# Convolution, MLP and GELU on one core: the 512-token blocks moved from two 64x128 TensorE tiles to four 64x64 tiles, with W_out stationary and the result transposed by VectorE

## The chip, the cores and the metric

One core of a Trainium2 chip. The metric is the device time of one execution in microseconds (us). All runs were correct, unless it is said otherwise, and of the fast state but for one each in the medians of e1 and e2. A ratio is the mean time of one kernel's fast runs over the mean of the other's from the same rounds, so it isn't quite the ratio of the medians quoted beside it.

## The reference

```python
# x: (8, 4096, 192), weight: (8 heads, 7 taps); softmax over the taps
w = softmax(weight, axis=-1)
out = einsum('hk,bskhg->bshg', w, causal_windows(x, 7))   # 24 channels per head
t = out.reshape(32768, 192)
h = t @ w_in                                              # 192 -> 2048
g = 0.5 * h * (1 + erf(h / sqrt(2)))
return g @ w_out                                          # 2048 -> 192, float32
```

## The kernel before

The tokens run in two halves of 16,384: half 0 lives on partitions 0 to 63, half 1 on 64 to 127, and the two row tiles of TensorE (64 rows each) work side by side. A block is 256 (six small ones at the start) or 512 tokens (29 blocks) of *each* half. VectorE transposes the input and does the seven taps for all blocks but two, two blocks ahead of their use. TensorE runs the first product of block n interleaved with the second product of block n-1; ScalarE does the Gelu.

```python
WS = [256] * 6 + [512] * ((HALF - 1536) // 512)     # block sizes
hp = [pst("hp%d" % i, [128, 2 * TB]) for i in range(2)]   # first product, 2 x 2 PSUM banks
ob = [pst("ob%d" % i, [128, 1024]) for i in range(2)]     # second product, 2 x 2 PSUM banks

def mm1(n, i):              # 128 of the 2048 hidden channels: 3 passes over 64 input channels
    ...
    for p in range(NP):
        for hf in range(2):                          # the two row tiles
            r = slice(64 * hf, 64 * hf + 64)
            ins = t.matmul(hp[u % 2][:, hf * TB + cc * w : ...],       # out: 128 x 512
                           win[r, p * F + wcols(hf, f0) : ... + 128],  # stationary 64 x 128
                           xc[n % 2][r, p * TB : p * TB + w],          # streamed 64 x 512
                           start=(p == 0), stop=(p == NP - 1), tile_position=(64 * hf, 0))

def mm2(m, g, ph, i):       # 4 groups of 2 x 128 tokens, 2 phases, 16 hidden chunks
    ...
    for hf in range(2):
        sub = ph ^ hf                                # row tiles swap banks between phases
        ins = t.matmul(ob[gg % 2][:, 512 * sub : 512 * sub + C],
                       gT[m % 2][r, c0 : c0 + 128],                    # stationary: tokens
                       wout[r, CH[i] * C : (CH[i] + 1) * C],           # streamed: 192 columns
                       start=..., stop=..., tile_position=(64 * hf, 0))

for i in range(NSL[n]):     # a slot: one piece of mm1(n), then its share of mm2(n - 1)
    mm1(n, i)
    for un in todo[a0:a1]: mm2(n - 1, *un)

def evac(e, m, g):          # VectorE: tensor_copy of 128 x (2 x 192) from ob to osb
def store(e, m):            # 4 DMAs per block, pieces of 3072 bytes
```

## Time and profile before

| | before |
|---|---|
| device time, median of 3 | 691.83 us (691.72 to 692.56) |
| span of the profiled run | 690.5 us |
| share busy: TensorE, VectorE, ScalarE | 99%, 80%, 77% |
| TensorE instructions (weight loads + matmuls) | 2 x 11,652 |
| steady 512-block, start to start | 20.92 us |

A group line of the profile gives the source line, the engine, the operation, output <- inputs, the shapes, how often; then total busy time and the mean of one in ns; then idle time before it and what ended it. A timeline line is start, length, engine, line, what, how many merged. Durations of matmuls overlap: what a matmul costs TensorE is the distance to the next start.

### The profile page before, as it was taken

Reading aid. Unit: us, or ns where it says so; the run is one execution under the profiler, and the core shown is the slowest. Engines: PE = TensorE matmul, PEld = TensorE weight load, DVE = VectorE, ACT = ScalarE, POOL = GpSimd, SP = SyncE. Lnnn points to the kernel's source line nnn. Section 1 sums busy time; section 2 is a strip of 40 time slices with the busy share of each in tenths; the row PEclk is TensorE's granted clock in tenths of the full one; section 3 lists DMA queues with packets and bytes.
Section 4 is the critical chain, followed back from the end, with each engine's and each line's share of the span. In section 5 each row is a group of like instructions: output and inputs, shape, how many; then the busy total and the mean of one; then the engine's idle time right before and its main releaser. Section 6 shows DMA issues by size and latency. Waiting matters only on the chain.

```text
span 690.5 us, 25644 instructions
## 1 busy us (share of the span) xinstructions
PE 682.3 (99%) x11652; PEld 506.3 (73%) x11652; DVE 555.7 (80%) x942; ACT 532.0 (77%) x536; POOL 45.1 (7%) x97
## 2 busy tenths in 40 slices
PE   8999999999999999999999999999999999999997
PEld 4899667777777777777777777777777777777777
DVE  6999977788977779878789777789877798777701
ACT  6788987777777777777777777777777777777771
POOL 7110000000000000000000000000000000000000
PEclk9999999999999999999999999999999999999999
DMA  9667844335554345653345553355544356521023
GB/s 198 134 149 165 205 111 109 88 88 132 138 137 100 74 106 138 139 135 88 82 112 138 138 122 87 84 124 138 138 101 93 86 136 139 135 50 40 11 48 93
DMA packets 24236, 78.15 MB, mean 113 GB/s; under 512 B 7232, under 2 KB 12480, under 8 KB 20416
## 3 DMA queue, kind: packets, MB, share of 16 engines
q1 hardware_dynamic: 19600, 72.24, 44.9%
q0 software_dynamic: 3792, 3.50, 2.9%
q8 instruction: 91, 1.49, 1.0%
q10 hardware_dynamic: 736, 0.78, 0.4%
q14 instruction: 17, 0.14, 0.1%
HBM read 52.90 MB, written 25.17 MB: 113 GB/s over the span
## 4 chain that ended last, share of the span: by engine, by line
PE 95%; DMA 2%; ACT 1%; POOL 1%; issue 0%; DVE 0%
PE ob L647 48%; PE hp L615 46%; DMA wout<-in_moe_w_out_dram 1%; ACT gT L547 1%; DMA xin<-in_x_dram 1%; POOL xin L204 0%; POOL xTb L302 0%; ACT osb L194 0%; ACT L496 0%; DVE osb L196 0%; DVE xT L413 0%
## 5 line engine op out<-in xcount | busy, mean ns | idle before, releaser
L547 ACT ACTIVATE gT<-hp 128x1024 bf16<-128x1024 f32 x512 | 522.8, 1023 | 139.7 <-PE hp L615 139.7
L647 PEld LDWEIGHTS ob<-wout,gT 64*128 64x128 bf16 x8192 | 352.7, 94 | 112.8 <-DMA wout<-in_moe_w_out_dram 1.3
L647 PE MATMUL ob<-wout,gT 64*128 64x192 bf16 x8192 | 420.7, 243 | 1.2 <-DMA wout<-in_moe_w_out_dram 1.1
L615 PE MATMUL hp<-xc,win 64*128 64x512 bf16 (+1 forms) x3360 | 415.5, 358 | 1.0 <-ACT gT L547 0.7
L443 DVE SCALAR_TENSOR_TENSOR acc<-xT,wcol,acc 128x512 f32<-128x512 f32 (+1 forms) x495 | 318.7, 710 | 0.0
L615 PEld LDWEIGHTS hp<-xc,win 64*128 64x128 bf16 x3360 | 154.6, 94 | 61.0 <-ACT gT L547 1.9
L196 DVE COPY osb<-ob 128x384 f32<-128x384 f32 x116 | 63.9, 551 | 124.2 <-PE ob L647 124.2
L443 DVE SCALAR_TENSOR_TENSOR xc<-xT,wcol,acc 128x512 bf16<-128x512 f32 (+1 forms) x99 | 65.1, 713 | 0.0
L413 DVE STREAM_TRANSPOSE xT<-xin 128x512 f32<-128x512 f32 (+1 forms) x105 | 61.3, 635 | 2.9 <-issue 2.1
L308 POOL COPY xT<-xT 128x558 f32<-128x558 f32 x33 | 21.5, 652 | 587.5 <-DVE xT L413 587.5
L436 DVE TENSOR_SCALAR acc<-xT,wcol 128x512 f32<-128x512 f32 (+1 forms) x99 | 56.2, 619 | 1.1
L291 POOL COPY xT<-xT 128x18 f32<-128x18 f32 x30 | 11.5, 384 | 1.1 <-DVE xc L396 1.1
L560 PE MATMUL hp<-warm 128*128 128x512 bf16 x16 | 5.4, 516 | 1.3 <-DVE warm L328 1.3
L576 PE MATMUL ob<-xTb,dg 64*64 64x256 bf16 x84 | 5.3, 271 | 1.1 <-ACT xTb L510 1.0
L576 PEld LDWEIGHTS ob<-xTb,dg 64*64 64x64 bf16 x84 | 4.3, 106 | 2.3 <-ACT xTb L510 1.5
L194 ACT ACTIVATE osb<-ob 128x384 f32<-128x384 f32 x12 | 5.8, 486 | 0.0
L560 PEld LDWEIGHTS hp<-warm 128*128 128x128 bf16 x16 | 1.9, 126 | 4.3 <-issue 2.4
L204 POOL DMA_DIRECT2D xin<-in_x_dram x10 | 5.0, 513 | 0.0
L258 POOL DMA_DIRECT2D win<-in_moe_w_in_dram x6 | 3.9, 655 | 0.0
L373 DVE COPY win<-win 64x768 bf16<-64x768 bf16 (+1 forms) x6 | 3.2, 532 | 0.2
L510 ACT ACTIVATE xTb<-xT 128x256 bf16<-128x256 f32 x3 | 1.1, 417 | 2.9 <-DVE xT L413 2.9
L302 POOL CAST xTb<-xT 128x186 bf16<-128x186 f32 x6 | 2.4, 402 | 2.7 <-DVE xT L413 2.7
(29 smaller groups left out, 14.1 us busy)
## 6 DMA issues: line engine op xcount, KB each, us to landing
xin<-in_x_dram SPq DMA_DIRECT2D x116, 380.0 KB, 6.8
out_dram<-osb SPq DMA_DIRECT2D x112, 192.0 KB, 3.0
out_dram<-osb SPq DMA_DIRECT2D x56, 48.0 KB, 2.2
xin<-in_x_dram SPq DMA_DIRECT2D x12, 188.0 KB, 3.9
xin<-in_x_dram POOLq DMA_DIRECT2D x10, 188.0 KB, 5.8
wout<-in_moe_w_out_dram POOLq DMA_DIRECT2D x1, 768.0 KB, 10.3
win<-in_moe_w_in_dram POOLq DMA_DIRECT2D x4, 96.0 KB, 4.4
win<-in_moe_w_in_dram POOLq DMA_DIRECT2D x2, 192.0 KB, 4.8
```

Of the source, the lines that this page charges most:

```text
L194: e.activation(out=dst, in_=src, func=AF.Copy).then_inc(S_EVA)
L196: e.tensor_copy(dst, src).then_inc(S_EV)
L291: g.tensor_copy(dst, ap(xT[(n - 1) % 2], WS[n - 1] + 31, [[NP * XW, 128], [XW, NP], [32, HB]],),).then_inc(S_HALO)
L308: g.tensor_copy(ap(t, 1, [[NP * tw, 128], [tw, NP], [32, HB], [1, 31]]), ap(t, WS[n], [[NP * tw, 128], [tw, NP], [32, HB], [1, 31]]),).the ...
L413: v.transpose(ap(xT[n % 2], p * XW + HL, [[NP * XW, 128], [1, w]]), ap(xin[n % NX], 64 * p, [[TB // 32 * D, 128], [D, w // 32], [1, 32]],) ...
L436: ins = v.tensor_scalar(a, src, wk, None, ALU.mult)
L443: ins = v.scalar_tensor_tensor(dst, src, wk, a, op0=ALU.mult, op1=ALU.add)
L547: a.activation(out=ap(gT[n % 2], i * c * 2 * w, dst), in_=ap(hp[u % 2], 0, src), func=AF.Gelu,).then_inc(S_GELU)
L560: t.matmul(hp[1][:, 0:512], warm[:, 0:128], warm[:, :])
L576: ins = t.matmul(b[r, o : o + w], dg[r, d0 : d0 + 64], xTb[PC[n]][r, x0 : x0 + w], start=(k == KS - 1), stop=(k == 0), tile_position=(64 * ...
L615: ins = t.matmul(hp[u % 2][:, hf * TB + cc * w : hf * TB + cc * w + w], win[r, p * F + wcols(hf, f0) : p * F + wcols(hf, f0) + 128], xc[n ...
L647: ins = t.matmul(ob[gg % 2][:, 512 * sub : 512 * sub + C], gT[m % 2][r, c0 : c0 + 128], wout[r, CH[i] * C : (CH[i] + 1) * C], start=(ph == ...
```

## The change

In the second product the roles swap for blocks 6 to 33: W_out becomes stationary (64 hidden x 64 output channels, every third channel), and 512 tokens are streamed through it. Four 64x64 tiles run at once: two row tiles (hf) by two column tiles (h, the token half). The result has channels on partitions, so VectorE evacuates it with a 32x32-block transpose into the row layout. The first product of blocks 7 to 34 is cut into 64-column tiles as well, so that the mode of the array stays the same. Four PSUM banks become a ring. The intent is to stream 512 columns instead of 192 per weight load. Below, a pair is the two matmuls that start together on two tiles, a quad the four on four tiles.

```diff
+            fw = 64 if M0 < n <= M1 else 128
+            for fo in range(0, 128, fw):
+                ins = t.matmul(
+                    hp[u % 2][fo : fo + fw, o : o + w],
+                    win[r, f1 : f1 + fw], ...
+                    tile_position=(64 * hf, fo),
 ...
+        UPLO = [(1, 0), (0, 2), (2, 1)]           # pass -> output third of each row tile
+            def mm2_t(m, ps, i):                  # 3 passes x 16 hidden chunks
+                if i == 0: ...                    # a bank of the ring must be free
+                for hf in range(2):
+                    j = UPLO[ps][hf]
+                    for h in range(2):
+                        ins = t.matmul(
+                            bank(ring(m, j), slice(64 * h, 64 * h + 64), w),
+                            ap(wout, 64 * hf * NF * C + CH[i] * C + j,
+                               [[NF * C, 64], [NP, 64]]),          # every third channel
+                            gT[m % 2][r, c0 : c0 + w],             # 512 tokens
+                            ..., tile_position=(64 * hf, 64 * h),
+            SHARE = [3, 3, 3, 3, 4, 3, 3, 3, 3, 4, 3, 3, 3, 3, 2, 2]
 ...
+        def evac_t(v, m, j):
+            v.transpose(
+                ap(osb[m % 2], j, [[8 * C, 128], [C // 2, TB // 32], [NP, 32]]),
+                bank(ring(m, j)),
+            ).then_inc(S_EV)
+        # places in VectorE's program: (n + 2, 18), (n + 3, 6), (n + 3, 9)
 ...                                               # store: pieces of 3072 -> 384 bytes
+                        [[mb * C, 32], [C, mb], [1, C // 2]],
 ...                                               # Gelu reads and writes in plain order
```

## The prediction

> **What bounds the kernel now.** I read the page first (busy shares, slices, chain of waits, groups), then the timeline of one steady block on PE and on VectorE.
>
> ```profile
> PE 682.3 (99%) x11652; PEld 506.3 (73%) x11652; DVE 555.7 (80%) x942; ACT 532.0 (77%) x536; POOL 45.1 (7%) x97
> ...
> PEclk9999999999999999999999999999999999999999
> ...
> PE 95%; DMA 2%; ACT 1%; POOL 1%; issue 0%; DVE 0%
> PE ob L647 48%; PE hp L615 46%; DMA wout<-in_moe_w_out_dram 1%; ACT gT L547 1%; DMA xin<-in_x_dram 1%; POOL xin L204 0%; POOL xTb L302 0%; ACT osb L194 0%; ACT L496 0%; DVE osb L196 0%; DVE xT L413 0%
> ```
>
> TensorE is the bound from end to end: 95% of the chain, halved between the first product (hp, L615) and the second (ob, L647), at a granted clock of 9 tenths or more in every slice. A busy PE is not a PE at its peak, so the question is whether there is waste between its starts. The groups give the shapes, the timeline the rhythm:
>
> ```profile
> L647 PE MATMUL ob<-wout,gT 64*128 64x192 bf16 x8192 | 420.7, 243 | 1.2 <-DMA wout<-in_moe_w_out_dram 1.1
> L615 PE MATMUL hp<-xc,win 64*128 64x512 bf16 x2784 | 376.3, 376 | 0.1
> ```
>
> ```profile
> 406.13 0.82 PE L647 MATMUL ob<-wout,gT 64*128 64x192 bf16 x16
> 406.79 0.81 PE L615 MATMUL hp<-xc,win 64*128 64x512 bf16 x6
> 407.44 0.82 PE L647 MATMUL ob<-wout,gT 64*128 64x192 bf16 x16
> 408.10 0.81 PE L615 MATMUL hp<-xc,win 64*128 64x512 bf16 x6
> ```
>
> Here the starts matter, not the durations (matmuls overlap). 16 second-product matmuls occupy 0.66 us: they run as pairs on the two row tiles, so 8 pairs at 82.5 ns. Six first-product matmuls occupy 0.65 us: 3 pairs, and the trace's single starts stand 216 ns apart. These two shapes separate rate and overhead: 320 more columns take 133.5 ns more, 0.417 ns a column (2.4 columns per ns), and what is left is 82.5 - 192 x 0.417 = 2.5 ns per pair. So TensorE already streams one column per cycle without holes; its only waste is 2.5 ns per pair: 3% of the second product, 1.2% of the first. A steady 512-block is 16 slots of 0.648 + 0.660, 20.93 us; block starts in the trace are 20.92 us apart, 27 times running.
>
> ```profile
> 405.03 1.02 ACT L547 ACTIVATE gT<-hp 128x1024 bf16<-128x1024 f32 x1 [0.28 <-PE hp L615]
> 406.34 1.02 ACT L547 ACTIVATE gT<-hp 128x1024 bf16<-128x1024 f32 x1 [0.28 <-PE hp L615]
> ```
>
> ```profile
> 416.00 3.39 DVE L443 SCALAR_TENSOR_TENSOR acc<-xT,wcol,acc 128x512 f32<-128x512 f32 x5
> 419.31 2.07 DVE L443 SCALAR_TENSOR_TENSOR xc<-xT,wcol,acc 128x512 bf16<-128x512 f32 x3
> 421.30 0.55 DVE L196 COPY osb<-ob 128x384 f32<-128x384 f32 x1
> 425.30 0.56 DVE L196 COPY osb<-ob 128x384 f32<-128x384 f32 x1 [3.45 <-PE ob L647]
> ```
>
> ScalarE waits 0.28 us for PE before each Gelu. VectorE has the convolution for the next block done at 421.4 and then waits 3.45 us for PE's last group: about 3.7 us of slack per block. Neither sets the pace.
>
> **What the Trainium skill says.** "TensorE: Matmul & The Clock Gate", section "Wait — 56ns, not 53.3ns?", gives N/2.4 + about 2.5 ns per warm matmul; the trace agrees (216 and 82.5 ns), and shows that two tiles side by side pay it once per pair. "TensorEngine Tiling (Array Packing)", sections "Tiling Modes" and "Gotcha 2", lists 64x64 as four independent tiles, says that a change of mode drains the engine, and that column tiling excludes Fast Weight Load. The trace before has 64x64 only in the opening convolution, two tiles of four: 107 ns a weight load against 94 at 64x128. When weights of one tile were loaded twice after a pause, the second load began about 28 ns after the first at 64x64, 15 ns at 64x128; I take these as the real occupancy of the load. The first page also says (Part 3, "The mechanism") that a load overlaps a running matmul only in another row group. The trace disagrees: in the second product each load starts 2 ns after the same row tile's matmul and the next still starts at 82.5 ns. "DMA: Bandwidth & Descriptors", "Specifications", puts line rate at 512 bytes or more a piece; the new stores are 384.
>
> **The change part by part.** It touches PE blocks 7 to 34, 28 of them.
>
> Second product. Removed per block: 4 groups x 2 phases x 16 chunks = 128 pairs with 192 columns, 128 x 82.5 = 10.56 us. Added: 3 passes x 16 chunks = 48 quads with 512 columns. If four tiles pay 2.5 ns once, 48 x 216 = 10.37 us. The streamed columns are the same (128 x 192 = 48 x 512), so this exchange saves only overhead: 80 x 2.5 = 0.20 us a block.
>
> First product. 48 pairs become 48 quads: 48 x 216 again. Nothing gained; it keeps the mode constant.
>
> Weight loads. A quad needs four of 64 columns in 216 ns; even wholly serial, 4 x 28 = 112 ns (estimate), hidden. Instructions to feed: 8 per 216 ns, 27 ns each, against 4 per 82.5 ns, 21 ns each, which the queue sustains today.
>
> VectorE. Removed: 4 copies x 551 = 2.20 us. Added: 3 transposes out of PSUM. The 512-wide transpose in SBUF took 680; PSUM source and steps of three words on the write side add something, I take 0.75: 2.25 us. Even. What moves is when it waits: the first transpose of a block stands before the last six convolution steps of the next input, and waits for pass 2. By the new shares pass 2 ends with slot 9: 10 x 0.648 + 32 x 0.216 = 13.4 us into the block, so 7.3 us remain. Signal 0.25 + transpose 0.75 + six steps at about 0.68 (3.39/5) = 5.1 us. Slack falls from 3.7 to about 2.2 us, still off the path. A bank is also free in time: pass 2 of the next block needs the second transpose, 6.9 us into that block; VectorE is there after 0.75 + six steps + three transposes and three first taps (3.6) + 0.7, about 9 us after pass 2 ended, 2 us into the block.
>
> ScalarE. Same 1023 ns; it reads plainly now. The tightest slots have two quads of the second product: 0.648 + 0.432 = 1.08 us, still over 1.02, and only twice per block.
>
> Stores. Per block 4 x 64 pieces of 3 KB become 4 x 512 of 384 bytes. The trace's W_out load is 2048 packets of 384 bytes at a median 51 ns: 2048 x 51 / 16 = 6.5 us of each engine per block, replacing 256 x 210 / 16 = 3.4. DMA share goes from about 0.48 to 0.63. Loads have over a block to land.
>
> Ends. One drain at each mode change, below 0.5 us. The last block's second group needs banks that two late transposes must clear: about 1.6 us after the passes end against 1.3 us of other work, some 0.3 us lost.
>
> Sum: 28 x 0.20 = 5.6 us saved, 0.3 to 0.5 given back, 5.2 net: 691.8 - 5.2 = 686.6, 0.75% faster.
>
> **The rivals.** (1) Four tiles don't stream freely: loads in a shared row group hold the neighbour's matmul, or the 2.5 ns is paid per column tile. For: no run here has two column tiles at once, and Fast Weight Load is lost. Against: loads hide in the same row tile at 82.5 ns, a tighter spot. 2.5 ns more per quad x 96 quads x 28 = 6.7 us, which just eats the gain (about 693); one exposed load of 28 ns per quad gives 75 us (about 760). (2) VectorE becomes the bound, if the transpose with steps of three words writes at half rate, 1.2 us each: the deadline becomes 5.6 of 7.3 us, still met, about 687. It takes 2.9 us per transpose to break it; at 3.5 us, TensorE would lose 0.6 us a block, about 17 us. (3) DMA: 160 ns per store packet would be 20 us per block, beyond capacity beside the loads, and the kernel would stretch to some 27 us a block (over 850). Packets of 768 bytes on the same kind of queue took some 47 ns, so I hold this for very unlikely. (4) Slow issue of stores with 512 pieces: SP waits 18 us in most blocks and could absorb several us per store.
>
> **Range and chances.** The gain has a hard ceiling: only overhead can go, so below 685 there is hardly anything, and 2% (678) would need 14 us where all the second product's overhead is 28 x 0.32 = 9 us. The failures are one-sided and mostly large. Predicted 686.6 us, range 685.0 to 696.0; faster by over 2%: 0.02, within 2%: 0.88, slower by over 2%: 0.10.
>
> **What would show it.** Right: block starts 20.72 us apart; 512-column matmuls in fours, quads 216 ns apart; PE idle as small as now; VectorE waiting some 2 us per block, at the transposes; DMA share near 0.6. Wrong: quads over 218 ns apart (rival 1); PE waiting for VectorE at a block's start (rival 2); transposes waiting on stores, or VectorE on loads of x (rival 3).

## The result and the profile after

| | before | after |
|---|---|---|
| device time, median of 4 | 691.78 us | 687.21 us (686.39 to 687.63) |
| ratio | | 0.9932 (0.9914 to 0.9949) |
| span of the profiled run | 690.5 us | 685.8 us |
| steady block, start to start | 20.920 us | 20.720 us |
| TensorE instructions | 2 x 11,652 | 2 x 12,548 |

The change is 0.7% faster, within 2%. The outputs are right. The page of the changed kernel, the lines that answer to those of before (busy shares; chain by line; the groups of both products, of the new weight loads and of the transposing evacuation):

```profile
PE 677.9 (99%) x12548; PEld 409.1 (60%) x12548; DVE 563.0 (82%) x914; ACT 532.0 (78%) x536; POOL 45.3 (7%) x97
...
PE hp L681 47%; PE ob L745 42%; PE ob L712 5%; DMA wout<-in_moe_w_out_dram 2%; ACT gT L610 1%; DMA xin<-in_x_dram 1%; POOL xin L256 0%; POOL xTb L366 0%; ACT osb L225 0%; ACT L556 0%; DVE osb L245 0%; DVE osb L227 0%; DVE xT L476 0%
...
L681 PE MATMUL hp<-xc,win 64*64 64x512 bf16 (+2 forms) x6048 | 418.5, 366 | 1.0 <-ACT gT L610 0.7
L745 PE MATMUL ob<-gT,wout 64*64 64x512 bf16 x5376 | 366.3, 376 | 0.0
...
L745 PEld LDWEIGHTS ob<-gT,wout 64*64 64x64 bf16 x5376 | 172.1, 118 | 123.0
L245 DVE STREAM_TRANSPOSE osb<-ob 128x512 f32<-128x512 f32 x84 | 74.0, 883 | 104.4 <-PE ob L745 104.4
```

TensorE is still the whole chain (47 + 42 + 5%) and still never idle in the steady part. What changed is the rhythm. The timeline of the changed kernel on TensorE:

```profile
405.68 0.82 PE L681 MATMUL hp<-xc,win 64*64 64x512 bf16 x12
406.33 0.82 PE L745 MATMUL ob<-gT,wout 64*64 64x512 bf16 x12
406.98 0.82 PE L681 MATMUL hp<-xc,win 64*64 64x512 bf16 x12
407.62 1.03 PE L745 MATMUL ob<-gT,wout 64*64 64x512 bf16 x16
```

Twelve matmuls, three quads, take 0.65 us from start to start: 216 ns a quad, for both products; the second product's slot was 0.66 us before. In the single starts of the trace every steady block is 20.720 us apart, 26 times in a row, against 20.920: 0.200 us a block.

VectorE in the same stretch of the changed kernel:

```profile
415.40 0.91 DVE L245 STREAM_TRANSPOSE osb<-ob 128x512 f32<-128x512 f32 x1 [3.00 <-PE ob L745]
416.18 2.01 DVE L506 SCALAR_TENSOR_TENSOR acc<-xT,wcol,acc 128x512 f32<-128x512 f32 x3
418.10 2.07 DVE L506 SCALAR_TENSOR_TENSOR xc<-xT,wcol,acc 128x512 bf16<-128x512 f32 x3
```

It waits 3.0 us for pass 2, transposes, and has the next input ready at 418.10 + 2.07 = 420.17; the block that needs it starts at 422.52. The slack is 2.35 us, where it was 3.72.

### The profile page after: what moved, and what is told of

The parts are those of the page before. It is cut to its first block, busy times and chain, and to the rows that moved or that the text cites. A ratio compares the mean times of both kernels' runs of the same rounds, so it can differ in the third digit from the quotient of the medians.

```text
span 685.8 us, 27314 instructions
## 1 busy us (share of the span) xinstructions
PE 677.9 (99%) x12548; PEld 409.1 (60%) x12548; DVE 563.0 (82%) x914; ACT 532.0 (78%) x536; POOL 45.3 (7%) x97
## 3 DMA queue, kind: packets, MB, share of 16 engines
q8 instruction: 98, 1.61, 1.1%
## 4 chain that ended last, share of the span: by engine, by line
PE 94%; DMA 2%; ACT 1%; POOL 1%; issue 0%; DVE 0%
PE hp L681 47%; PE ob L745 42%; PE ob L712 5%; DMA wout<-in_moe_w_out_dram 2%; ACT gT L610 1%; DMA xin<-in_x_dram 1%; POOL xin L256 0%; POOL xTb L366 0%; ACT osb L225 0%; ACT L556 0%; DVE osb L245 0%; DVE osb L227 0%; DVE xT L476 0%
## 5 line engine op out<-in xcount | busy, mean ns | idle before, releaser
L681 PE MATMUL hp<-xc,win 64*64 64x512 bf16 (+2 forms) x6048 | 418.5, 366 | 1.0 <-ACT gT L610 0.7
L745 PE MATMUL ob<-gT,wout 64*64 64x512 bf16 x5376 | 366.3, 376 | 0.0
L506 DVE SCALAR_TENSOR_TENSOR acc<-xT,wcol,acc 128x512 f32<-128x512 f32 (+1 forms) x495 | 314.1, 699 | 0.0
L681 PEld LDWEIGHTS hp<-xc,win 64*64 64x64 bf16 (+1 forms) x6048 | 187.7, 106 | 135.6 <-ACT gT L610 2.1
L745 PEld LDWEIGHTS ob<-gT,wout 64*64 64x64 bf16 x5376 | 172.1, 118 | 123.0
L245 DVE STREAM_TRANSPOSE osb<-ob 128x512 f32<-128x512 f32 x84 | 74.0, 883 | 104.4 <-PE ob L745 104.4
L712 PE MATMUL ob<-wout,gT 64*128 64x192 bf16 x1024 | 52.2, 243 | 1.7 <-DMA wout<-in_moe_w_out_dram 1.4
L712 PEld LDWEIGHTS ob<-wout,gT 64*128 64x128 bf16 x1024 | 43.6, 94 | 7.9 <-DMA wout<-in_moe_w_out_dram 1.7
L227 DVE COPY osb<-ob 128x384 f32<-128x384 f32 x4 | 2.2, 558 | 7.8 <-PE ob L712 7.8
```

The lines of the kernel that those rows point to most:

```text
L245: v.transpose(ap(osb[m % 2], j, [[8 * C, 128], [C // 2, TB // 32], [NP, 32]]), bank(ring(m, j)),).then_inc(S_EV)
L506: ins = v.scalar_tensor_tensor(dst, src, wk, a, op0=ALU.mult, op1=ALU.add)
L681: ins = t.matmul(hp[u % 2][fo : fo + fw, o : o + w], win[r, f1 : f1 + fw], xc[n % 2][r, p * TB : p * TB + w], start=(p == 0), stop=(p == N ...
L712: ins = t.matmul(bank(bb[sub], w=C), gT[m % 2][r, c0 : c0 + 128], wout[r, CH[i] * C : (CH[i] + 1) * C], start=(ph == 0 and i == 0), stop=( ...
L745: ins = t.matmul(bank(ring(m, j), slice(64 * h, 64 * h + 64), w), ap(wout, 64 * hf * NF * C + CH[i] * C + j, [[NF * C, 64], [NP, 64]],), g ...
```

## The experiments

Twelve kernels ran with the kernel before beside them. Medians (e1 and e2 each hold one run classed as slow, 843.34 and 743.92 us; the medians of their fast runs are 833.41 and 731.78; the ratios are of fast runs alone):

| run | time, us | ratio to before |
|---|---|---|
| e0_after: the changed kernel again | 686.78 | 0.9930 |
| e1_old64: old roles on four tiles | 835.55 | 1.2063 |
| e2_split256: first product in quads of 256 | 732.07 | 1.0560 |
| e3_split128: first product in quads of 128 | 1004.06 | 1.4536 |
| e4_mm1_128: first product left on 64x128 | 796.73 | 1.1521 |
| e5_dense_evac: transposes write side by side (wrong result) | 687.20 | 0.9935 |
| e6_plus2: two more transposes | 686.98 | 0.9930 |
| e7_plus4: four more transposes | 705.08 | 1.0192 |
| e8_before384: before, stores written as 384-byte pieces (they moved as 3072 all the same) | 692.00 | 1.0001 |
| e9_half256: half of the slots cut as in e2 | 697.99 | 1.0085 |
| e10_idle192: one added wait instruction per matmul of the first product | 908.99 | 1.3141 |
| e11_idle384: two added wait instructions | 1441.29 | 2.0832 |

The theory: only the fixed 2.5 ns per pair or quad was saved. The rivals: the four tiles themselves bring the gain; the waits and VectorE bring it; or other parts of the change cost something that hides a larger gain.

**e0_after.** No edit.

> The changed kernel itself once more, for a tighter ratio and as the yardstick of this call. Theory (only the fixed cost per matmul quad was saved, 80 quads of 2.5 ns in each of 28 blocks): 687, ratio 0.993. If the first result had been chip luck, the ratio would drift towards 1.000 (no gain) or below 0.990.

686.78 us, 0.9930 (0.9918 to 0.9942). The result stands.

**e1_old64: four tiles, old roles.** On the kernel before:

```diff
-  ob[gg % 2][:, 512 * sub : ... + C], gT[m % 2][r, c0 : c0 + 128], ..., tile_position=(64 * hf, 0)
+  for h in range(2):
+    ob[gg % 2][64 * h : 64 * h + 64, 512 * sub : ... + C],
+    gT[m % 2][r, c0 + 64 * h : c0 + 64 * h + 64], ..., tile_position=(64 * hf, 64 * h)
   # and the first product cut the same way, as in the changed kernel
```

> The kernel before, with every matmul cut into two 64-column tiles, but the old roles kept: tokens stationary, 192 columns of W_out streamed; 128 quads of 82.5 ns per block, so as many fixed costs as before. Theory (the four tiles themselves bring nothing, the longer stream does): 691.8, within 0.3%. Rival A (four tiles as such are the gain): about 687. Rival B (weight loads of the four tiles run one after another, some 28 ns each, 112 ns against 82.5 ns of streaming): 128 x 30 ns = 3.8 us more per 512-block, near 800 us. If only the two loads of a row group are serial (56 ns) they stay hidden and nothing shows.

835.55 us: far off, and at first sight rival B. The timeline of this kernel on TensorE says otherwise:

```profile
401.39 0.66 PE L650 MATMUL ob<-wout,gT 64*64 64x192 bf16 x22
405.59 0.43 PE L650 MATMUL ob<-wout,gT 64*64 64x192 bf16 x10 [3.55 <-issue]
...
406.44 0.90 PE L650 MATMUL ob<-wout,gT 64*64 64x192 bf16 x32
407.10 0.89 PE L617 MATMUL hp<-xc,win 64*64 64x512 bf16 x12
407.75 0.90 PE L650 MATMUL ob<-wout,gT 64*64 64x192 bf16 x32
```

Where it runs, 32 matmuls (eight quads of 192 columns) take 0.66 us and the first product 0.65, exactly the pace of the kernel before. So serial weight loads of the four tiles are excluded, and the four tiles alone don't shorten anything either: the theory's reading holds in these stretches. But in the middle of a slot TensorE stands still for 3.55 us, and the profile names no wait ("issue"). I hadn't expected that. Something outside the array limits this kernel; more of it below.

**e2_split256 and e3_split128: more quads for the same columns.** On the changed kernel:

```diff
-  for p in range(NP):
+  cw = 256 if M0 < n <= M1 else w            # e3: 128
+  for x0, p in [(x0, p) for x0 in range(0, w, cw) for p in range(NP)]:
       ...
-      hp[...][fo : fo + fw, o : o + w], win[...], xc[...][r, p * TB : p * TB + w]
+      hp[...][fo : fo + fw, o + x0 : o + x0 + cw], win[...], xc[...][r, p * TB + x0 : p * TB + x0 + cw]
```

> The changed kernel with each 512-column quad of the first product (blocks 7 to 34) cut into two of 256 columns: same columns, same result, 48 more quads per block. Theory (2.5 ns per quad): 48 x 2.5 x 28 = 3.4 us more, 690.6. Rival C (the gain came from the schedule of waits or from VectorE, and the count of quads is free): no change, 687. Rival D (each tile pays its own fixed cost): 10 ns per quad, 13 us more, 700.

> The same with four quads of 128 columns: 144 more quads per block, 144 x 2.5 x 28 = 10.1 us more, 697. A quad streams 53 ns; two serial loads of a row group (56 ns) would just begin to show, some 192 x 3 ns x 28 = 15 us further (712); four serial loads (112 ns) would add 192 x 57 x 28 = over 300 us. Rival C: no change.

732.07 and 1004.06 us: both missed. Again the trace splits in two. Blocks of e2 without a pause are 20.840 us apart (two of the 27 distances are 20,840 ns and one is 20,847): 0.12 us more than 20.720, which is 48 quads x 2.5 ns to the nanosecond. That confirms the term that carries the prediction. In unpaused slots of e3, 48 matmuls of 128 columns (12 quads) take 0.67 us, 55.8 ns a quad, so four weight loads are hidden even there. That 1004 us is close to what four serial loads would have given by the expectation (697 plus over 300) is chance: these slots rule it out. The rest is pauses. The waits of e2 (engine, what, waited for, total us, times, longest):

```profile
PEld hp L682 <- issue: 23.9, 21, 3.8
PE hp L682 <- issue: 18.1, 13, 3.5
PEld ob L746 <- issue: 12.7, 12, 3.8
PE ob L746 <- issue: 8.5, 7, 3.5
```

Counting TensorE instructions (weight loads and matmuls) in the trace between one pause over 0.43 us and the next gives distances such as 1021, 256, 1021, 1277, 1021 in e2, and 254 to 256 or a multiple in all 167 distances between the 168 such pauses of e3. The 21 such pauses of e2 sum to 33.4 of the 44 us it lost. Five of the six pauses of e2 that lasted 2.4 us or more also have a drop of the granted clock to 0.5, for 3.4 us, within 1.1 us of their end (mean granted clock 0.988 in e2, 0.94 in e3). Now look at the page's line for the queue that carries instructions (packets, MB, share of 16 engines). The kernel before:

```profile
q8 instruction: 91, 1.49, 1.0%
```

The changed kernel:

```profile
q8 instruction: 98, 1.61, 1.1%
```

e2:

```profile
q8 instruction: 140, 2.29, 1.4%
```

e3:

```profile
q8 instruction: 224, 3.67, 1.5%
```

A packet is 1.61 MB / 98 = 16.4 KB, and 98 x 256 = 25,088 is the count of TensorE's weight loads and matmuls (25,096); 140 x 256 = 35,840 against 35,848 in e2. So this queue brings TensorE's program in packets of 256 instructions. The Trainium skill says the same ("Runtime: NRT & Kernel Launch", "Instruction fetch mechanics": refills in 16 KiB blocks of 256 instructions), and adds that the fetch is hidden. It isn't in e1, e2 and e3: the kernel before used a packet every 20.92 x 256 / 704 = 7.6 us, the changed one every 6.9; e2 would need one every 4.6, e1 every 3.8, e3 every 2.8. They got one per 730 / 140 = 5.2 us in e2, 826 / 181 = 4.6 us in e1 and 999 / 224 = 4.5 us in e3, on average over the run.

The traces also hold the start and the end of each packet of this queue, and they settle the question. Number all TensorE instructions of a trace in order, semaphore instructions too. The 251 pauses over 0.43 us in e1 (55), e2 (21), e3 (168) and e9 below (7) all end at an instruction whose number leaves the same remainder, 193, when divided by 256; from one pause to another the packet that landed last moves on by exactly one per 256 instructions; and it had landed 1.2 to 1.7 us earlier. The 27 pauses of e7 below, which wait for the convolution, are spread over all remainders. So TensorE stood waiting for its next 256 instructions. In the steady part of the changed kernel the packet that came closest landed 2.9 us before the instruction that needed it (1.4 to 3.0 us in e0, e5, e6 and e7, which run the same TensorE program), in the kernel before 1.8 us, and no pause followed.

**e9_half256: is the supply the reason?** As e2, but only in odd slots:

```diff
-  cw = 256 if M0 < n <= M1 else w
+  cw = 256 if M0 < n <= M1 and i % 2 else w
```

> The changed kernel with the 512-column quads of the first product cut in two in every second slot only: 24 more quads and 192 more TensorE instructions per block, 960 where the changed kernel has 768 and the fully cut one 1152. In the fully cut kernel the blocks without a pause took 20.84 us, as 2.5 ns per quad says, and the rest was pauses of up to 4 us, each 255 or a multiple of it instructions after the last. New theory (TensorE's instructions arrive in batches of 256, and a batch comes about every 4.3 to 4.9 us at best): 960 per block is one batch per 5.5 us, so no or hardly any pauses, and what is left is 24 x 2.5 ns: blocks of 20.78 us, 1.7 us more than the changed kernel, 688.6. Rival (cut quads as such make the array pause): half of the 45 us that the full cut added, near 709.

697.99 us against the 688.6 of the supply theory and the 709 of its rival. 18 of the 27 steady blocks took 20.78 us (20.779 to 20.790), as 24 x 2.5 ns says. In the other nine there were pauses, up to 4.6 us in one block; seven were over 0.43 us, and all six distances between them were multiples of 255 to 256 instructions (semaphore instructions aren't counted, so a few short of 256 each). So the mark of the packet stays, and cut quads as such don't pause. But the limit is softer than I put it: even at a packet per 5.5 us some come late. The traces show two cases. In e3 the packets themselves are the limit: they start a median of 3.8 us apart where one per 2.8 is needed, and 111 of the 168 late ones come with the 16 DMA engines under 0.2 busy with other queues in the 2.5 us before. In e2 and e9 the late packets meet other traffic: before all 28 of them that share was 0.68 or more, while over the steady part fewer than half of the packets (38% and 45%) saw as much. No run varied that traffic alone, so the second case is a reading of traces and not an experiment.

**e10_idle192 and e11_idle384: the same number of instructions without more matmuls.** On the changed kernel:

```diff
+  if M0 < n <= M1:
+      for _ in range(3):                     # e11: 4; in the trace one mostly rides on the weight load, two fit one instruction
+          t.wait_ge(S_WARM, 1)               # reached long ago
   ins = t.matmul(hp[u % 2][fo : fo + fw, o : o + w], ...
```

> The changed kernel with one more instruction ahead of each matmul of the first product, a wait on a semaphore that has long been reached: 192 more TensorE instructions per block, 960, but no more matmuls or weight loads. New theory (supply of instructions, enough at 960): 687 as the changed kernel. Rival (the queue itself is slowed by such instructions): several us more even here.

> The same with two such waits per matmul: 1152 instructions per block, the total (35,963) equal to that of the fully cut kernel, with the quads of the changed kernel. New theory (supply): pauses again at distances of about 256 instructions, and a time near the fully cut kernel less its 3.4 us, 715 to 735. Rival (the weight loads or short matmuls of the four tiles made the pauses): 687.

909 and 1441 us: inconclusive for what they were made for. The waits themselves slow TensorE: blocks grew from 20.72 to about 28.4 and 47.6 us, 40 ns per added instruction in e10, 70 in e11. The rival noted for e10 is right, and the times say nothing of the supply. What they do show is what a packet holds: with no more matmuls or weight loads than the changed kernel, e11 took as many packets as e2, and e10 121:

```profile
q8 instruction: 140, 2.29, 0.7%
```

And e10, which needs only one packet per 7.5 us, still has six pauses over 0.43 us, all with the remainder 193 and with other queues on 0.70 or more of the DMA engines just before: the mean pace isn't all that counts. A probe that adds instructions free of cost I don't have.

**e4_mm1_128: why recut the first product?** On the changed kernel:

```diff
-  fw = 64 if M0 < n <= M1 else 128
+  fw = 128
```

> The changed kernel with the first product left on 64x128 tiles, so that only the second product is changed and the tile mode switches twice per slot, 32 times per block. In the changed kernel's trace the two places where the mode switches show about 0.09 us between starts beyond the usual. Theory (each switch drains the array, about 0.09 us): 28 x 32 x 0.09 = 81 us more, near 768. Rival (a switch is free, the first product was recut for nothing): 687.

796.73 us. The timeline on TensorE:

```profile
405.25 0.86 PE L745 MATMUL ob<-gT,wout 64*64 64x512 bf16 x12
406.04 0.82 PE L681 MATMUL hp<-xc,win 64*128 64x512 bf16 x6
406.79 0.86 PE L745 MATMUL ob<-gT,wout 64*64 64x512 bf16 x12
```

0.79 and 0.75 us in place of 0.65 and 0.65. Blocks are 24.653 us apart: (24.653 - 20.720) / 32 = 0.123 us for each change of tile mode, somewhat more than the 0.09 I had taken (at block 7 of the changed kernel the second quad after the change is 0.024 us late too). Here the pauses can't be the reason: this kernel has fewer TensorE instructions than the changed one, and the delay is in every slot. The recut of the first product gains nothing by itself, but without it the change would lose 15%.

**e5_dense_evac: what does the transpose pay for?** Wrong results on purpose:

```diff
-  ap(osb[m % 2], j, [[8 * C, 128], [C // 2, TB // 32], [NP, 32]])
+  ap(osb[m % 2], j * TB, [[8 * C, 128], [32, TB // 32], [1, 32]])
```

> Wrong results on purpose: the three transposes out of PSUM write their 512 words side by side instead of in steps of three words, all else the same. It splits the 883 ns of a transpose into source and writing. I took 750 in the prediction. If the steps of three cost it, it falls to about 700 to 750 ns (the PSUM source alone over 680 in SBUF); if the PSUM source costs it, it stays near 880. The time should stay at 687 either way, since VectorE isn't on the path.

687.20 us, as expected, and the group of the transposes in this kernel reads:

```profile
L245 DVE STREAM_TRANSPOSE osb<-ob 128x512 f32<-128x512 f32 x84 | 59.2, 707 | 112.3 <-PE ob L745 112.3
```

707 instead of 883 ns. So the PSUM source costs 707 - 680 = 27 ns over the transpose in SBUF, and writing in steps of three words 176 ns. None of it is on the path.

**e6_plus2 and e7_plus4: how much slack has VectorE?**

```diff
   if j == 0:
+      for k in range(2):                     # e7: 4
+          v.transpose(dump[:, :], bank(ring(m, j)))   # each waits for the one before
```

> The changed kernel with two more transposes into an unused buffer ahead of the first transpose of each changed block: some 1.7 us more on the path from pass 2 to the next block's input. VectorE's slack there is about 2.3 us by the trace, so theory: still 687. Rival (VectorE is already at the edge): each extra transpose shows, 28 x 1.7 = 48 us more.

> The same with four: some 3.4 us more against 2.3 us of slack, so TensorE must wait about 1.1 us at the start of each changed block: 28 x 1.1 = 30 us more, 710 to 725. If it stays at 687, the slack was larger than I read it; if e6_plus2 also rises, smaller.

With two: 686.98, nothing. With four: 705.08, a little under what I expected, and TensorE waits for the convolution. The waits of e7 (engine, what, waited for, total us, times, longest):

```profile
PE hp L689 <- DVE xc L514: 12.9, 27, 0.5
```

The extra transposes write side by side and took about 0.72 us from start to start, not 0.85; four are 2.9 us. Blocks are 21.39 us apart, 0.67 more, and the input is ready 0.15 us before its first matmul, which is then the delay of the signal. The usable slack is therefore 2.35 - 0.15 = 2.2 us, and 2.9 - 2.2 = 0.7 us is what shows.

**e8_before384: do small stores cost?** On the kernel before:

```diff
-  [[mb * C, 32], [HALF * C, 2], [1, j * C]]
+  [[mb * C, 32], [HALF * C, 2], [C // 2, 2 * j], [1, C // 2]]
```

> The kernel before with its stores cut into pieces of 384 bytes, eight times as many, as the changed kernel writes them; same rows, same result. Theory (the stores have slack): 691.8 as before, ratio 1.000 within 0.002. Rival (the small pieces cost the changed kernel part of its gain): one or two us more, 693 to 694.

692.00 us, 1.0001 (0.9988 to 1.0013), as the theory said, but the run tests nothing: the pieces follow each other without a gap on both sides, and the trace shows that they were moved as before, 7168 packets of 3072 bytes. Its page has the same line as the kernel before, word for word:

```profile
DMA packets 24236, 78.15 MB, mean 113 GB/s; under 512 B 7232, under 2 KB 12480, under 8 KB 20416
```

The changed kernel, which does write 384-byte packets (57,344 of them):

```profile
DMA packets 74418, 78.25 MB, mean 114 GB/s; under 512 B 64576, under 2 KB 69824, under 8 KB 70592
```

That small stores cost nothing rests on the changed kernel alone: no computing engine waits for a store in its trace (only the queue of SyncE does, 1.5 us, where it was 1.6 before), and its steady blocks are 20.720 us with nothing beside the 96 quads.

## Why the prediction was right, point by point

- **The bound** stayed TensorE, and no new wait appeared in a steady block.
- **The exchange of 128 pairs for 48 quads**, 0.20 us a block: measured 20.920 to 20.720, 0.200. e2 and e9 confirm the 2.5 ns per quad by adding quads (20.840 and 20.780 in unpaused blocks). That four tiles pay it once was the open point; 216 ns a quad settles it. e1's unpaused slots show that the four tiles bring nothing without the longer stream.
- **The first product**: nothing gained, kept for the mode. e4 puts a price of 0.123 us on each change of mode it avoids.
- **Weight loads and Fast Weight Load** (rival 1): hidden, even with 56 ns quads in e3. One reading under it was loose: the opening convolution of the kernel before does use two column tiles at once, in different row groups; what no run had was two in one row group.
- **Instructions to feed**: here the prediction was incomplete. It compared the short-term pace (27 against 21 ns) and didn't count the supply over a block, which is 9% more instructions than before. The changed kernel stays below the limit, but e9 with 960 per block already doesn't always, so the margin that I took for granted is under a quarter in mean pace. That the change stayed inside it was luck: the prediction didn't look.
- **VectorE**: the transpose was put at 0.75 us and takes 0.88; the slack was put at 2.2 us and is 2.35 by the trace, 2.2 usable by e7; VectorE waits 3.0 us at the first transpose, where I forecast some 2. The transpose reading of e5 says why the first number was low: the steps of three. The second transpose is needed 7.3 us into the next block by the trace, where I wrote 6.9; it is done long before.
- **Stores**: I took 51 ns a packet and a DMA share of 0.63. In the trace a 384-byte store packet takes a median of 28 ns, and the share over the steady stretch is 0.50 (0.48 before): the packet was taken almost twice too dear, from a load on another queue, without a wait that shows. (The 210 ns for the old packets is a mean; their median is 238.)
- **Ends**: in the single starts, the last block's second group came 0.30 us late (386 ns after the matmul before it, where 83 are usual), as predicted for the late banks. The mode change at the start of block 7 and the one before the tail show 0.09 and 0.10 us.
- **The sum**: 28 x 0.20 = 5.6 us less 0.3 to 0.5 gives 686.6; measured 687.21 and 686.78. The profiled pair differs by 4.7 us, because block 7 of the changed kernel began at 90.97 instead of 90.38 us. 0.09 of these 0.6 us is the mode change; the rest differs from run to run (89.46 to 90.97 in the five profiles of after, e0, e5, e6 and e7; 90.38 and 90.16 in before and e8). From the start of block 7 to the end the pair differs by 5.3 us (600.1 and 594.8), which is 5.6 less 0.3.

## What to carry to other kernels

When TensorE's starts leave no gap but the fixed cost, as here, swapping roles that keep the streamed columns can only save that cost: count the pairs or quads saved, multiply by the 2.5 ns measured here, and that is the ceiling. Keep one tile mode through the inner loop, since a change cost 0.12 us each time in e4. Before cutting matmuls into more and shorter ones, count TensorE's instructions per microsecond: one packet of 256 every 6.9 us was fine here, every 5.5 us no longer always. And check in the trace that an edit did what it was written for: e8 looked like a clean result and had changed nothing.

## What the Trainium skill lacked or had wrong

- "Runtime: NRT & Kernel Launch", "Instruction fetch mechanics", calls the fetch mostly hidden. With short matmuls it wasn't: pauses of up to 6.2 us at distances of 254 to 256 TensorE instructions or a multiple in e3, one packet per 4.5 us on average there, and single late packets already at one per 5.5 us (e9). The page doesn't say how long a packet takes: TensorE went on 1.2 to 1.7 us after one had landed.
- "TensorE: Matmul & The Clock Gate", Part 3, "The mechanism", lets a weight load overlap a running matmul only in another row group (its list of what overlaps; the text above that list also allows a load into the background weight buffer, and the traces fit this). Loads into the same row tile stayed hidden at 82.5 ns per pair (before) and at 55.8 ns per quad of four tiles (e3).
- The same page gives 2.5 ns per matmul; that in a steady stream four tiles side by side pay it once (216 ns a quad of 512 columns) isn't there.
- "TensorEngine Tiling (Array Packing)", "Key Properties", says that a change of mode drains the engine, without a figure: 0.123 us a change in e4.
- "DMA: Bandwidth & Descriptors", "Specifications", asks for 512 bytes or more for line rate. Stores to HBM in pieces of 384 bytes took a median of 28 ns a packet, 0.073 ns a byte, no more per byte than the 3 KB pieces before (238 ns, 0.077). The DMA engines were half idle in both (share 0.50 and 0.48), so this isn't a test at line rate.
- "SBUF — State Buffer", "Door 1: The DMA port swizzle", names up to four fp32 as a stride that is free, though it also asks for two accesses to each 16-byte line, which steps of three words give only in part. A transpose of 512 words that writes in steps of three words took 883 ns, and 707 side by side (e5).
- No page found gives the price of wait instructions for a semaphore long reached, in TensorE's queue: 40 ns per added instruction in e10 and 70 in e11, where a further wait rode on each weight load.
